# Own-block masks on two engines, and a new order, in a four-layer attention kernel

## The chip, the cores and the metric

The kernel runs on one core of a Trainium2 chip. The core has TensorE (PE, with a weight loader that the profile lists as PEld), VectorE (DVE), ScalarE (ACT), GpSimd (POOL) and SyncE (SP, which here only issues DMAs); they run side by side and meet through semaphores. The metric is the time of one execution on the device in microseconds (us). Before the change three runs gave a median of 410.37 us (410.02 to 410.41).

## The reference

The input has 2048 tokens of 512 features in bfloat16. Four residual layers follow each other: A, B, A, B, all with 32 heads of 16 features, and each with a layer normalisation ahead of it.

```
x = x + A(layernorm(x), A_wqkv, A_wo)      # twice, in turn with
x = x + B(layernorm(x), B_wqkv, B_wo)

A: phi(t) = where(t > 0, t + 1, exp(t)) + 1e-6
   kv = sum_s phi(k)_s v_s ;  z = sum_s phi(k)_s
   o = phi(q) kv / (phi(q) z + 1e-6) ;  o @ wo

B: scores = q k^T * 16^-0.5, kept where 0 <= i - j < 256, else -1e9
   o = softmax(scores) v ;  o @ wo
```

A is linear attention over the whole sequence: nothing can be read from it before all keys have been summed. B is causal attention over a window of 256 tokens. A score outside the window ends as a probability of zero, and these zeros are what the changed lines make.

## The kernel before

**Tiles.** Tokens are cut into 16 tiles of 128. The residual `xres` stays on the chip through all layers. Matrix products go into the eight banks of the accumulator `PS` (`ps` in the profile), and ScalarE or VectorE bring them out.

**Stages.** `layer_a_keys` builds the first layer's key sums; `barrier` closes a linear layer; `middle(2)` runs the end of the first A layer, the first B layer and the start of the second A layer tile by tile; a second `barrier` follows; `middle(3)` runs the end of the second A layer and the second B layer, and stores the result. Inside a `middle` the steps of tile j+3's projections, tile j's scores and tile j's values stand side by side.

**A normalisation** (`norm`) is a chain over engines: mean and variance on VectorE (L367, L368), an epsilon added on GpSimd or VectorE (L369), the power -1/2 on GpSimd (L370), the normalised tile on VectorE (L371), then a transpose, mostly by a DMA of SP's queue (L377), and then the projections on TensorE (L406, L420), whose results are evicted by ScalarE or VectorE (L395, and L591/L592 for the keys). In the linear layers the exponential of `phi` is ScalarE's (L429) and its clamp and join are VectorE's (L430, L431).

**A sliding-window tile.** `b_scores` is called four times for each key tile j: for two halves b of 64 keys and two groups of feature blocks `fs`. TensorE multiplies the keys with up to 256 queries (L638), in four row groups of 32 and four banks; ScalarE takes the exponential of two banks at a time into the probabilities `pb` (slots in `vp` in the last stage) (L648). The first 64 queries of each such block overlap the keys' own positions, so part of them must be zero: the mask `mk` does this, by a product with the 0/1 triangle `tri` on VectorE (L656), in place, over 8 head rows of 64 columns for 128 keys. `b_far` treats the 64 queries at the window's far end (L677, L680 on TensorE, L690 on ScalarE); its mask `mf` covers 16 head rows and is made by VectorE's product (L709) or by GpSimd's `affine_select` (L708), which writes zeros where an affine function of partition and column is negative. In the last B layer (`merged`) the own and far blocks of tiles 0 to 13 share their columns; there the own mask is made in `b_far` on VectorE (L700), and `b_scores` masks only tiles 14 and 15. `b_values` multiplies the probabilities with the values (L729) for three key tiles at a time; it reads `pb` after all masks. Its sums are divided (L740, L741), transposed and projected, and added to the residual (L574).

**The order.** Nothing is ordered at run time. `Plan` lists 2542 operations with their dependences and, for some, the engines that may run them (`g.add(name, {engine: cost, ...})`). `place` unpacks `TABLE`, which holds three things found by a search made beforehand: a place in the order for every operation, the engine of every operation, and the accumulator bank of every tile. Each engine then plays its operations in that order and waits at each on semaphores of the others. `place` also adds waits: a bank's new user waits for the old ones, and a longer GpSimd operation waits for the last VectorE operation of the kinds in `WIDE` that stands before it:

```
SHORT = ("eps", "pow", "c2", "c2b", "c11", "c12", "c13", "c14")
WIDE = ("E1", "xn", "mk", "mf")
...
        if o.eng == "POOL" and o.name not in SHORT and wide and wide not in o.deps:
            o.deps.append(wide)
        if o.eng == "DVE" and o.name in WIDE:
            wide = o
```

`synchronise` lets every GpSimd operation wait for the one before it on GpSimd. Output stores `outp` (L847) go through SP's or GpSimd's queue, as the table says. Ten matrix products without use (`fill`, L268) and nine more at the very start (L984) keep TensorE busy while the first tiles come in.

Of the kernel before, what the change touches and what calls it, by code (L numbers as in the profile page):

```python
# [218 lines left out]
def bass_view(x, free):  # L219

    return bass.AP(x.tensor, x.offset, [x.ap[0]] + free)


class Plan:
# [398 lines left out]
    def b_scores(self, j, b, fs, key):  # L623

        K = self
        ps = [Tile(1, "S") for _ in range(4)]
# [15 lines left out]
        sl = j % self.rp  # L642
# [8 lines left out]
        if skip:  # L651
            return

        def mk(e):
            x = bass_view(K.P(sl)[:, fs[0], 0, 384 * b:384 * b + 64], [[704, 4 * n], [1, 64]])
            return e.tensor_tensor(x, x, K.tri[:, 0, :].unsqueeze(1).to_broadcast([P, 4 * n, 64]), ALU.mult)  # L656
# [200 lines left out]


TABLE = (
    r"c-qZa1K1|VvaT*P*0yciwr$(CZQHhO+qTW@CcDXcb7%hV<eVfoo0F4!@AKUGhSk+o?^{*fGyMUCh3765goc+c9E6835CI|rLPAiG2oggihztY|-3#}`C",  # L860
    r"4r=n43a|>hzijl3kWoa6p#`avO+fK1uY;ujD@Ez2SkS$&>LDpE9e8oAQe1v8a6_D$N)JZ7i0tjaUd=@c<fq38+hjCLu%LreIXx=gZ!`=YC|392gRX3jE",
    r"8s-6Ba;xXbbJY!USjp?I9C9aCKn-420Zp80tY9=m1@zK6Hc3&>dnyIY<i)AUHIJK`<CP!bC^_O<)o%ghj9zmcUi$1Y4j7Y=t3k1dhTn*aop79W;b4Py#",
    r"x`WOxo!U?>cOGEf$#LQi-BFJUPxgXItmuE7^L4%guZOoQoA9lpZPumWzvN{Fjw!EBfV!=XHU2d|(4Y=<4N6L!H|m;p0kHSC5}a023~lW+<^DHU4HgD@(",
    r"-N}%?_Ew~MLpedY&Gw>S1syz@+B~;(TS-1;7z#BLZ;Z=H72~d$@RTG*)26YbZ!F?D3BViO&1yK*+Eo4-gR3epF{Rlrn1Qk(5QUz5ZRaj+KSyU3G)k84K",
    r"s>rH{DypKWf=~#mKvb1fy@O;bxpFGH8VzHhw#urqsbVU-%Aty@5~`$%rgEyvkW!^kxl}1tTIE({RaI3@l~Gkx0jQ($KwhY;>Zt~*vZ}6XsFtdgYOQLjT",
    r"B^QU18ZR&6ow*D6xyhUs;z3I8mo4yiE6K!tBTN6HB&9rde{Ip-~#M}{cr#}sDm(CjZq=s5j=*uYM!bFW7Rk{QjJm<VVxSU)~iEM5+<mLYQDMzlhgur85",
    r"XJ|s-xPVp1@O>tlq;1n4)H=nQE3=q&BL>YKfYvrm5+wlez+%)Mm9`9aRU^QuPcvt1fDeI;OU$t?Hm!sk*9<uu9c})vBB7u0FvswOj?m;J8A~R=3n~6#|",
    r"2);OdSl1t-)=bxQS6Au$wQRoB#QbzN;!C9ouZhSMs9I;;+<N9wUEh1*p~6-t%H&=>}HsGaJGx~ZaL42+4-)C<*9mBF&OOYK(A)jf4zmBTZtmkNt})LB&",
    r";o~m=|fm)+3sEg{nTB~AX0!)Mn@uez{XYirAq-tU<ysK`gI2aG(Vr@K&=WrCB#|wB7M`IEkgYj{nN`|RaYV}UNS0B_H^-;Z5KdPTpQcR8^AsnVr;V}Y^",
    r"#c?<uBVt;W0uy5etcaDcGVWE8FeRo_bulug!i*RN>){oZ2`{S&I1w9Q6|9Q&F*9bt)OZPF;bp9Y)$o&QhAnV5&cV6Z96zf`_(gqHKP$jS*ch{7Hq4GW@",  # L870
    r"Gf4#?^Hv)hxf4wHpN#;AtK>xH5q?UQ*bJ_!mHQ@b7E_}hS#y2`d;-`jOA5Zte`5YN-7Q3z+9LXJ7X8@iVH9uw#0>)8@pk5%z$|?FXlr*jZrZ_7QjUq4H",
    r"u(9i%YNv&PRvKuqRH#7-}h|$CxUX>V*YyIZnqJ7+b|rE3go*!mYRsx8n|6iG5UGRUOyhIxLL+)Bx2RS7U!w1jEr<T#rSu7>1_^R2(BxB#KP)@EJbG7kC",
    r"4A;x62cd+-N*gEz4<RiU?d3m@SVe29;+5B9~ExEG^PRLY~OQa_AFc~yTLfcaE@)ebx0U7CdhaS%Sm0_q;M$4)pHhv1JGpAt|)x=#buAoU%-#u?NRXJR#",
    r"~PBo||?Zf@}3OC?Jyn_dDCVj%sIEyyn_qYXXQ40EkUvW0gp`Q^bB`HEmMX4zX#iH1hjN;Hx9ENGAHXX#Il$?g+2poy&XfAEW=oEuuQhjPb4=@8A!ozq3",
    r"(^5{#MYpjbJ)lhVkXlkkBFas9s1+rmN0gqJgftz+%(Rl)QXLwsT2mWpPl@RmKBgzMidIuQ>Oeo?dwhrSs4mr`yp)gf(+4a-9jOU5rB2kD3X-9&)Sa5qa",
    r"Xf(^@g#Pm=G2eYQGc38mK+76`LuxI(kVQR184&Ur$RK4TF`nbOkHRb^`IgYf{Icx8bpI>Ej^_nw3&v|7Ro|dX)6_{5>%2F(jr<+*=PxEqwTbmcF;1~NF",
    r"gZ{4N)W1P?eoRQy3~mKhPT*uHMoxwTpIB4%$PBI58*Tq@0Y`P-!YdWhpF`qsCO8l5+~~NiV4vrQ~NcjC#{|G@M4zNE$_r=oRgw*R-Gd&~y5p4$~2OL8I",
    r"v?9is#EiN4Sp9z$bkFYTnYypEgmJNiuTX&il}7Tl5#Q7S%8<LLyQq!08n0r&M@8mH(qt>?^~g@2-~oSJ{6kJO4=a~md3!)aNVIRuB~P@IF?a!wA-nhz3",
    r"kE<QtN=^UM>c07S5QXUS&VR;fwrYV$;^Ko7d$KkmM=jIEvfs1i|UQX$`D6gOl{3HLw@3=h|;6i+nE>UsL#+RuqZ{$rJfy;4cF3%OXAQ$G%+?Ts>f9}9t",
# [36 lines left out]


# [153 lines left out]
```

## Time and profile before

| | |
|---|---|
| median of 3 runs | 410.37 us |
| span of the profiled execution (the page gives no other time of it) | 408.2 us |
| TensorE busy | 396.0 us (97%) |
| VectorE busy | 347.9 us (85%) |
| ScalarE busy | 344.4 us (84%) |
| GpSimd busy | 113.8 us (28%) |
| own-block masks on VectorE (L656) | 72, 0.42 us each |
| far masks on GpSimd (L708) / on VectorE (L709) | 39 at 1.15 us / 17 at 0.69 us |

A row of the groups reads: line, engine, operation, what it writes `<-` what it reads (buffer numbers left out), shapes, count | busy us, mean ns of one | idle time of its engine just before these instructions, and which engine's work ended it. A row of the waits reads: who waited `<-` for whom, us in total, times, longest. A piece of the chain is its start, its length and what ran. The span runs from the first to the last instruction; matmul ends are modelled, so a busy TensorE may still have short gaps. Granted clock is 1.00 in every stage.

### The profile page before, as it was taken

To read this page: it belongs to the slowest core of one execution; us is meant where nothing else is said; L and a number is where in the kernel's file an instruction comes from. 1 tells how busy PE (TensorE), PEld (TensorE's weight loads), DVE (VectorE), ACT (ScalarE), POOL (GpSimd) and SP (SyncE) were. 2 spreads that over 40 slices of the span, in tenths; PEclk is the share of its full clock that TensorE was granted. 3 is DMA by queue.
4 is the path that set the end of the run, shared out by engine and by line. 5 is a ranking of instruction groups with operands and counts; after the bars stand their busy time and mean duration, and the time that the engine had idled before them with its cause. 6 is when DMAs were issued, how large, how long until landed. Compare 5 with 4: busy or idle time off the path is not lost.

```text
span 408.2 us, 18082 instructions
## 1 busy us (share of the span) xinstructions
PE 396.0 (97%) x7997; PEld 263.4 (65%) x7997; DVE 347.9 (85%) x808; ACT 344.4 (84%) x443; POOL 113.8 (28%) x194
## 2 busy tenths in 40 slices
PE   8999999999999999999999999999999999999996
PEld 3654676666575566666666777676757766576664
DVE  5998799999998999888977789988898778876685
ACT  3655579999999999999998355999998999999992
POOL 3553632112253343330503202122123201302212
PEclk9999999999999999999999999999999999999999
DMA  8754014923242934344231100364225542442543
GB/s 247 243 118 104 2 42 121 184 56 97 65 119 52 132 73 108 75 104 106 62 69 36 29 2 28 89 127 78 71 76 130 143 83 61 66 121 62 118 109 104
DMA packets 67654, 37.88 MB, mean 93 GB/s; under 512 B 48248, under 2 KB 62712, under 8 KB 67576
## 3 DMA queue, kind: packets, MB, share of 16 engines
q1 hardware_dynamic: 67184, 35.67, 38.1%
q8 instruction: 63, 1.03, 1.1%
q0 software_dynamic: 384, 1.05, 0.8%
q14 instruction: 15, 0.12, 0.1%
q10 hardware_dynamic: 8, 0.00, 0.0%
HBM read 6.29 MB, written 2.10 MB: 21 GB/s over the span
## 4 chain that ended last, share of the span: by engine, by line
PE 81%; ACT 10%; DVE 7%; DMA 1%; issue 1%; DVEq 0%
PE ps L406 27%; PE ps L420 20%; PE ps L729 15%; PE ps L638 8%; ACT pb L648 7%; PE ps L680 2%; PE ps L481 2%; ACT pb L690 1%; DVE XQ L563 1%; PE ps L677 1%; DMA XQ<-vp 1%; PE ps L984 1%; PE ps L457 1%; PE ps L543 1%; PE ps L268 1%
## 5 line engine op out<-in xcount | busy, mean ns | idle before, releaser
L648 ACT ACTIVATE pb<-ps 128x1024 bf16<-128x1024 f32 (+3 forms) x224 | 198.2, 966 | 7.4 <-PE ps L638 6.2
L729 PEld LDWEIGHTS ps<-vB,pb 128*128 128x128 bf16 x2560 | 77.6, 96 | 11.5 <-issue 4.2
L729 PE MATMUL ps<-vB,pb 128*128 128x34 bf16 x2560 | 83.2, 177 | 0.3
L420 PE MATMUL ps<-xT,wBp 128*128 128x128 bf16 x1024 | 68.6, 219 | 0.1
L420 PEld LDWEIGHTS ps<-xT,wBp 128*128 128x128 bf16 x1024 | 58.4, 98 | 9.6 <-issue 4.0
L708 POOL TENSOR_SCALAR_AFFINE_SELECT pb<-pb 128x1024 bf16<-128x1024 bf16 x34 | 39.1, 1149 | 84.0 <-DVE pb L700 31.9
L429 ACT ACTIVATE tE<-ps 128x512 bf16<-128x512 f32 x64 | 38.1, 606 | 18.4 <-PE ps L406 12.1
L638 PE MATMUL ps<-XQ,kB 32*128 32x256 bf16 (+2 forms) x1024 | 48.7, 262 | 3.3 <-ACT pb L648 0.6
L574 DVE TENSOR_TENSOR xres<-ps,xres 128x512 bf16<-128x512 f32 x63 | 43.1, 685 | 9.6 <-PE ps L406 9.1
L690 ACT ACTIVATE pb<-ps 128x1024 bf16<-128x1024 f32 x50 | 49.0, 1048 | 1.3 <-PE ps L680 1.0
L406 PE MATMUL ps<-wA,XQ 128*128 128x512 bf16 x192 | 49.2, 380 | 0.7 <-DMA XQ<-vp 0.6
L369 POOL TENSOR_SCALAR ve<-mv 128x1 f32<-128x1 f32 x49 | 11.8, 240 | 127.9 <-DVE mv L368 126.9
L370 POOL TENSOR_TENSOR rs<-ve,negh 128x1 f32<-128x1 f32 x64 | 37.9, 592 | 32.0 <-DVE ve L369 27.5
L367 DVE BATCH_NORM_STATS2 stats<-xres 128x6 f32<-128x512 bf16 x64 | 43.8, 685 | 2.8 <-DMA xres<-in_A_x_dram 2.1
L638 PEld LDWEIGHTS ps<-XQ,kB 32*128 32x128 bf16 x1024 | 15.7, 92 | 31.4 <-ACT pb L648 8.3
L420 PE MATMUL ps<-XQ,wA 128*128 128x128 bf16 x512 | 34.4, 219 | 0.0
L406 PE MATMUL ps<-wBv,xT 128*128 128x512 bf16 x128 | 34.3, 380 | 0.0
L406 PE MATMUL ps<-M,XQ 128*128 128x512 bf16 x128 | 33.3, 380 | 0.2
L420 PEld LDWEIGHTS ps<-XQ,wA 128*128 128x128 bf16 x512 | 30.1, 98 | 5.1 <-issue 0.6
L406 PE MATMUL ps<-wBo,oT 128*128 128x512 bf16 x124 | 32.7, 380 | 0.6 <-DVE vp L431 0.4
L656 DVE TENSOR_TENSOR pb<-pb,tri 128x512 bf16<-128x512 bf16 x68 | 27.7, 419 | 3.7 <-ACT pb L648 3.1
L741 DVE TENSOR_TENSOR o<-ps,rc 128x256 bf16<-128x256 f32 x64 | 27.0, 422 | 1.7
(114 smaller groups left out, 545.9 us busy)
## 6 DMA issues: line engine op xcount, KB each, us to landing
vB<-vS SPq DMA_DIRECT2D x64, 136.0 KB, 2.6
kB<-vp SPq DMA_DIRECT2D x64, 128.0 KB, 2.2
wA<-in_A_wqkv_dram SPq DMA_DIRECT2D x3, 512.0 KB, 5.2
xres<-in_A_x_dram SPq DMA_DIRECT2D x2, 512.0 KB, 4.8
pb<-in_B_wqkv_dram SPq DMA_DIRECT2D x1, 1024.0 KB, 6.9
out_dram<-xres POOLq DMA_DIRECT2D x8, 128.0 KB, 2.5
out_dram<-xres SPq DMA_DIRECT2D x7, 128.0 KB, 2.0
xres<-in_A_x_dram SPq DMA_DIRECT2D x3, 256.0 KB, 5.3
```

The costliest lines, as they stand in the source:

```text
L367: self.on("DVE", "stats", lambda e: e.bn_stats(K.stats[:, t, :], K.xres[:, t, :]), key, dve(512), rd=[("xres", t)], wr=[("stats", t)])
L370: self.pow = self.on("POOL", "pow", lambda e: e.tensor_tensor(K.rs[:, t, :], K.ve[:, t, :], K.negh[:], ALU.pow), key + 0.03, (640, 690), r ...
L406: m = e.matmul(K.ps(ps), lhs(c), rhs(c), start=c == 0, stop=c == 3)
L420: m = e.matmul(K.ps(ps)[:, f * P:(f + 1) * P], w(c, f), xT(c), start=c == 0, stop=c == 3)
L429: self.on("ACT", "E", lambda e: e.activation(K.tE[:, s, :], K.ps(ps), ACT.Exp, bias=0.0), key, act(512), wr=[("tE", s)], ps=[ps])
L574: self.on("DVE", "res", lambda e: e.tensor_tensor(K.xres[:, t, :], K.ps(po), K.xres[:, t, :], ALU.add), key, dve(512), rd=[("xres", t)], w ...
L638: m = e.matmul(K.ps(ps[gq])[:, ns * i:ns * i + ns], K.kB[rows, j % 4, 2 * f + b, :, :], K.XQ[rows, f, q:q + ns], start=True, stop=True, ti ...
L648: return e.activation(out(h, ns).rearrange("p (f g) c -> p f g c", f=n), i, ACT.Exp, bias=0.0, scale=0.25)
L656: return e.tensor_tensor(x, x, K.tri[:, 0, :].unsqueeze(1).to_broadcast([P, 4 * n, 64]), ALU.mult)
L690: return e.activation(o.rearrange("p (f g) b c -> p f g b c", g=2), i, ACT.Exp, bias=0.0, scale=0.25)
L708: return e.affine_select(out=x, in_=x, compare_op=ALU.is_ge, fill=0.0, base=-2, pattern=[[0, 16], [-2, 64]], channel_multiplier=1)
L729: m = e.matmul(K.ps(ps)[:, 34 * u:34 * u + 34], K.P((b // 2) % rp)[:, f, gq % 2 * 2 + gq // 2, o:o + P], K.vB[:, (b // 2) % 4, b % 2, r, : ...
```

## The change

The mask `mk` of `b_scores` may now be made on GpSimd too: there it is an `affine_select` in place, which keeps an element of the block where 1 + 2 x column - partition is not negative and writes 0 elsewhere, over the same 8 x 64 columns. Which engine makes a mask is read from the table, as for `mf`. The search's cost for it is 600 ns on GpSimd. The 56 own masks of `b_far` stay on VectorE.

The table is a new one: it has other places in the order, other engines for those operations that may go to several, and other banks. 50 of the 72 masks of `b_scores` go to GpSimd (46 of 64 in the first B layer, 4 of 8 in the last). Other operations that change engine: far masks (6 more on VectorE in the first B layer, 3 fewer in the last), epsilon adds, some evictions, a few clearings and weight copies of the start, and 2 output stores that go from SP's queue to GpSimd's. 439 of the 1007 accumulator tiles get another bank.

```diff
@@ b_scores
-        def mk(e):
+        def mk(e, eng):
             x = bass_view(K.P(sl)[:, fs[0], 0, 384 * b:384 * b + 64], [[704, 4 * n], [1, 64]])
+            if eng == "POOL":
+                return e.affine_select(out=x, in_=x, compare_op=ALU.is_ge, fill=0.0, base=1, pattern=[[0, 4 * n], [2, 64]], channel_multiplier=-1)
             return e.tensor_tensor(x, x, K.tri[:, 0, :].unsqueeze(1).to_broadcast([P, 4 * n, 64]), ALU.mult)
 
-        self.on("DVE", "mk", mk, key + 0.02, dve(256 * n, "2x"), rd=[("P", sl, f, b, h) for f in fs for h in range(2)] + [("tri",)], wr=[("P", sl, f, b, 2) for f in fs])
+        self.g.add("mk", {"DVE": dve(256 * n, "2x"), "POOL": (600, 660)}, mk, key + 0.02, rd=[("P", sl, f, b, h) for f in fs for h in range(2)] + [("tri",)], wr=[("P", sl, f, b, 2) for f in fs])
@@ TABLE
...
```

More of the change, by code (lines that the diff above doesn't have):

```diff
@@ L864 @@
[L864 to L879, printed above, removed]
@@ new lines @@
+    r"76gOZPzU-#KS%{_pe-DPb}$agKwTIQ?V&Stfv(UW2EZX$05M@8Y=AUSA3DGw*a$ITA#{Vma2QfUJ=g@B;Ujc{jxYp<!V!oA6Cf^hhly|*Ccz?D4DnzIOomU8",
+    r"2lB#axB^pP25f<?unmsFQkV%-VLEJwS@0B&!Bw~hm0=k?gXb^}Uchy@0m~tzdI>uKlv4Si0W^e_uoI5M2{;KW;3nLHP%5^%4X5B0po*hTLuj=dW<wYiR^5R)",
+    r"unX=&5hx17U^t{z`BfvR24|rZ#8vTB0Z69`LVT58y@odsPQ8V9K&lvMRUYm`0rdl9P^=QDGjI=#`Vqpbj4Fbv0K?T!5K)P;s-Q}!8bcvfSTzBsBB{tKkxHyG",
+    r"smv;iilRn9R+U60RYg=$RZJCEQB`s^5~@Nrm0cxMIaCQ%Qsso4s<bKxl~pNKNmWsyp{6Pgqo9_mt?H<Xs;a7{3PC;9T(wZuRSnfrt%B9C2691eC=9JsUDZ~t",
@@ new lines @@
+    r"h1RN}YNV<_eN`43sB_R%HCF4OojMO~R5R5?U4V<Q2lm29HA<C$lCTf<!)!H2jZmXibr_=_z(bg;#;S2@ys89;)M0f1=Bb}yf?A{2s`+Z7dJmVNy?O)-)IzmR",
+    r"EmDisBsEQSP}9{6HA_{5^=hWttB$D0&{6GElhuATMQu=>)CZWVp1=~dR4r2*)h5+NEmtelO0`*SQC(GMby@uaSJVx4R9#iKR5x`@9alHi3H2)kQ9)HO6$FD~",
+    r"F}$rFs7ERoo>W^^4LG2Js}QO<mcZb+O<h+H)pivXqhSa<sJg4iDmp$<*VHq$L+w;OR7os_tJEnK5?8C!DmdIxrSYkXfxFZhbynR~_tZI62FqehEQjaS1r-nP",
+    r"tDdSl*1%Jk0Apb&42?DMG={-5I0B!mkvIzDV?rE_DO4Oxgt74~rc`n9tvZMA)DNl_UQ|D+pVfQyK_$V&m`a7kaF`4uU_?BRKdSIp9xGsSOo3x?ERMrHsv_=I",
@@ new lines @@
+    r"zo^tIjY^M^@B&`MI#>_u;w4oZ>thD2gq1NPX2S8<1ZUzb{8fEaO)(`_!P(dh8(>5Hq&};pm>C-(U>3ZMS@DI+hIjBTzErQ2LPWv|I1wk|WNd*gu{pk0t?&|F",
+    r"#w*ww->5R`Dwb8{R4Po3X)ql&#`3BocESp39xlMnm>qNAd`yd7Fem21+?WURVm{Q!Xi#twF2SxCO<8mp1@mJ!?2e0Z3NFOxDu(KTQ*kLq#%UN+#Zt>~1un<U",
+    r"xCMKut+*1mVQ;kx`>6t05Z7QK?1`%}427k>YA*IsRWTeD#<lnapJEX#is2~&UBm6T1E1j=ypB6@7gnT7^cJh(4Sa`l@Hsxfhgg}a&=2?sdtq<vgMG0d=2E#;",
+    r"9u<)yQDka^?Ql27rFfKARi%6?3f-m|IF0(Nd)OZb;6SWK15{h=fRFJ7-l6Gqm*P`<oI%y;6~4sRxChtadfbcqa6kTn8*n53ipeNBeZ<fB34u0YBC0`y@Bkjf",
@@ new lines @@
+    r"6qJ$_Atk0mI2~h9Oo~N=aR|<&S(JqC<50YXsVEIarD!yp=Fl)4jy0(+)uW^ool;X;x{38E9o?h*^ni#CV|L0w=_w=Spq$j4T2KPg#FUE+C8U<ridxfhT0w2;",
+    r"2-c!D)Q(otj~JWc(9c+#>X1-w%0oY4Udl)LsXcX|qu7y-;c@It@3AX&p+?l0EIA57AFvP2r4x7(=g~kFl!8$c>PCHO4XvYQ)Q|d80V+s^s41<b4YZLu(Eu7q",
+    r"t7ttHrXp07Hc=+ZOvPvr4W=P9pNi80T1XG+5oMu8w1pPa63R+jX&Y^)H}sa?(I6F^2CEQMf_6|y8m5M*p=uZHq->NxC)9~_V!fG?=%hNCE=i^6F*TslRE8Q-",
+    r"cj`gU=>>(NC-jtt(n~5!J?R<kp<#584pDL)no{WDG=dJ(UK&ZSXdnGTAE_6urd7H(HPuJxS8AqzqMvCuHP@qPG>xILv|6vxN9h=SrnUMwouHGnPOsPR$$LrY",
@@ L915 @@
+    r"Kl*$Mit(RI_JuxF-?VSmqZELMzly+%?l%U}fOsJQ`#yZMzSzU*=gQOe{6ir6FM;}m`|Vgz2LvC8(AW3oS^2j<7lD5KX>SI#(q4+#kD1X6hsCQG_Q~=fdI=}v",
+    r"1?F9dR-QXe=wl_t+8CczKlMIXAGYrx5Qk^XOT1Sj{-rMngbo21{BXs`9~jN=3HKa&ZoMP~)Qt)}2U<W9-z;#TF@LS^$!F2K2lluK$W>rczf_Cz3f%uJfxt`$",
+    r"`U_m60v}!wU-L`-eOc>MPJZEf0drs>1gdy33V8k?Fi(NV0+D)2@?3c|2ZkA#W#6fvbKjo&QaXNJ{KmguBjSGv=r5)JdtC*X4yZHVN?`T;_5gU)egPZ^-;V{=",
+    r"Z)N@EDI_0>F9n}u{vVVdGBE",
 )
```

73 lines of the change are left out of this document (34 added, 39 removed).

## The prediction

> **What bounds the kernel.** I read the page first, its shares of engines and the chain, then the busy times by stage, then the chain piece by piece, and last the waits.
>
> ```profile
> span 408.2 us, 18082 instructions
> PE 396.0 (97%) x7997; PEld 263.4 (65%) x7997; DVE 347.9 (85%) x808; ACT 344.4 (84%) x443; POOL 113.8 (28%) x194
> PE 81%; ACT 10%; DVE 7%; DMA 1%; issue 1%; DVEq 0%
> ```
>
> The chain that ended last is 81% TensorE. The stages in turn (columns: length, busy time with instruction count for PE, PEld, DVE, ACT, POOL, then clock, DMA share and GB/s); 60 to 225 is the first sliding-window layer ("the second stage" below), 260 to 400 the last one:
>
> ```profile
> 0.00:60.00 60.00, 58.07 (x564) 34.10 (x565) 52.23 (x128) 32.26 (x54) 26.96 (x66) 1.00 0.45 126
> 60.00:80.00 20.00, 19.98 (x312) 13.54 (x310) 19.24 (x44) 18.84 (x24) 4.34 (x11) 1.00 0.71 153
> 80.00:220.00 140.00, 137.94 (x2898) 88.90 (x2896) 124.19 (x292) 136.84 (x160) 43.29 (x62) 1.00 0.39 85
> 220.00:260.00 40.00, 39.90 (x637) 28.83 (x636) 34.21 (x75) 22.39 (x41) 8.20 (x16) 1.00 0.13 32
> 260.00:400.00 140.00, 135.41 (x3492) 94.68 (x3489) 114.11 (x263) 132.57 (x165) 28.65 (x39) 1.00 0.42 93
> 400.00:408.20 8.20, 4.72 (x111) 3.34 (x109) 3.93 (x9) 1.46 (x4) 2.38 (x5) 1.00 0.42 130
> ```
>
> TensorE and ScalarE are both close to full in the two sliding-window stages; VectorE, which the change relieves, is third. TensorE's idle time can be read off stage by stage: 1.9 us to 60, 0.0 to 80, 2.1 to 220, 0.1 to 260, 4.6 to 400 and 3.5 in the tail. That is all that a better order could take out, since the changed program issues the same 868 TensorE steps. Two stretches of the chain show both limits:
>
> ```profile
> 1.25 4.02 PE ps L984 x9
> ...
> 115.54 3.77 ACT pb L648 x4
> 119.80 7.39 ACT pb L648 x8
> 127.19 1.83 ACT pb L690 x2
> 129.02 2.75 ACT pb L648 x3
> ...
> 143.76 0.34 PE ps L677 x32
> 144.11 1.45 PE ps L420 x24
> 145.56 0.86 PE ps L406 x4
> 146.42 0.34 PE ps L677 x32
> ```
>
> From 143.76 each TensorE piece begins where the one before it ends; at 115.5 to 131.8 it is the exponentials, with no mask between them. The busy time of a matmul counts its modelled tail, so short gaps don't show in the stage sums; I allow 3 us for these (an estimate of mine: the loader's waits below come in pieces of up to 0.7 us), which makes at most 2.1 + 4.6 + 0.7 + 3 = 10.4 us to be had, the 0.7 being what of the first 60 us is not the first 1.25 us before any work.
>
> **The change part by part.** In the changed program 50 of the 72 own-block masks are GpSimd selects, 46 of the 64 in the second stage and 4 of the 8 in the last. The order and engine choice of everything else comes from a new table too.
>
> ```profile
> L656 DVE TENSOR_TENSOR pb<-pb,tri 128x512 bf16<-128x512 bf16 x64 | 26.0, 418 | 3.5 <-ACT pb L648 3.1
> L708 POOL TENSOR_SCALAR_AFFINE_SELECT pb<-pb 128x1024 bf16<-128x1024 bf16 x24 | 27.6, 1151 | 44.2 <-ACT pb L690 19.1 <-DVE tE L430 10.3 <-DVE pb L656 8.3
> L328 POOL TENSOR_SCALAR_AFFINE_SELECT spread<-spread 128x512 bf16<-128x512 bf16 x4 | 3.4, 848 | 0.6
> L334 POOL TENSOR_SCALAR_AFFINE_SELECT tri<-tri 128x64 bf16<-128x64 bf16 x1 | 0.2, 238 | 1.1 <-DVE tE L430 1.1
> L709 DVE TENSOR_TENSOR pb<-pb,tri 128x1024 bf16<-128x1024 bf16 x4 | 2.7, 682 | 0.0
> L592 DVE CAST vp<-ps 128x512 bf16<-128x512 f32 x25 | 18.3, 730 | 4.3 <-PE ps L420 3.9 <-DMA kB<-vp 0.3
> L591 ACT ACTIVATE vp<-ps 128x512 bf16<-128x512 f32 x7 | 5.3, 755 | 2.6 <-PE ps L420 2.6
> L395 ACT ACTIVATE XQ<-ps 128x512 bf16<-128x512 f32 x10 | 6.0, 597 | 1.2 <-PE ps L420 0.8
> L369 DVE TENSOR_SCALAR ve<-mv 128x1 f32<-128x1 f32 x15 | 2.2, 149 | 0.3
> L847 POOL DMA_DIRECT2D out_dram<-xres x8 | 4.7, 594 | 22.3 <-DVE xres L574 13.8 <-DVE vp L656 5.5 <-DVE pb L700 3.0
> ```
>
> Masks off VectorE: 46 x 0.418 = 19.2 us less in the second stage, 4 x 0.418 = 1.7 us less in the last.
>
> Price of a select of 512 elements: not in the trace in this form. It lies between 0.24 us (64 elements) and 1.15 us (1024); the one row of 512 elements, with another pattern, has 0.85. A line through the two ends gives 0.24 + 448/960 x 0.91 = 0.66 us, and I take that, because the row of 1024 has the same kind of pattern and tile. GpSimd gets 46 x 0.66 = 30.4 us there (39 at the row of 512).
>
> Masks of the far blocks: 6 more go to VectorE in the second stage (+4.1 us there, 6.9 us off GpSimd), 3 fewer in the last (2.0 us off VectorE, +3.5 on GpSimd).
>
> Small moves in the second stage: 6 epsilon adds to VectorE (+0.9); key evictions, two more on VectorE (+1.5) and off ScalarE (-1.5); query evictions, one the other way (-0.7, taken at the key's size; +0.6 on ScalarE). Sum: VectorE -19.2 + 4.1 + 0.9 + 1.5 - 0.7 = -13.4 us, ScalarE -0.9 us, GpSimd about +22 us on the 52 it has there, still under half of 165. In the last stage VectorE loses about 5 us, ScalarE gains 1.4 us for two evictions (they stand near 274 and 311, where it is 1.2 us in 20 idle) and a 1.2 us clearing before it. Two output stores move from SP's queue to GpSimd's, at 0.59 us of it each, all but the last of them long before the end.
>
> The order: engine by engine, 693 of TensorE's 868 steps and 367 of ScalarE's 442 keep their relative order, and a TensorE step shifts by 1.2 places on average; TensorE changes between full and split arrays 333 times in both. So TensorE's work costs nothing more or less, and what can change is only its idle time.
>
> What covers the longer mask? The waits of TensorE's loader and of GpSimd, between 60 and 225 us (columns: total, times, longest):
>
> ```profile
> PEld ps L638 <- ACT pb L648: 5.1, 11, 0.7
> PEld ps L729 <- DVE pb L656: 1.0, 4, 0.3
> ...
> POOL ve L369 <- DVE mv L368: 54.0, 17, 9.4
> POOL pb L708 <- ACT pb L690: 19.1, 6, 6.1
> ```
>
> The probability-times-value matmuls (L729) waited four times for a mask, at most 0.3 us, so most masks are done early and 0.24 us more (0.66 against 0.42) is hidden; without that cover 46 x 0.24 = 11 us would show. GpSimd has the room: it sat 54 us waiting for nothing but the next mean and variance.
>
> The sum for the path: of the 2.1 us of idle TensorE in 80:220 I take half to go, since VectorE is the third engine there and loses 10% of its load; of the 3 us of hidden gaps 0.7; of the 4.6 us in 260:400 only 0.8, because the relief there is small and the last part of that stage runs on exponentials; against it 0.6 us for selects that hold VectorE up. -1.0 - 0.7 - 0.8 + 0.6 = -1.9 us. The profiled span of 408.2 becomes 406.3; the median of the runs, 410.37, stands 2.2 us above the span, and I keep that: **408.5 us**.
>
> **A row against the relief.** GpSimd and VectorE have held each other up once in plain sight:
>
> ```profile
> 37.57 0.85 POOL L328 TENSOR_SCALAR_AFFINE_SELECT spread<-spread 128x512 bf16<-128x512 bf16 x1
> ...
> 37.65 0.92 DVE L430 TENSOR_SCALAR tE<-tE 128x512 bf16<-128x512 bf16 x1
> ...
> L430 DVE TENSOR_SCALAR tE<-tE 128x512 bf16<-128x512 bf16 x64 | 18.4, 292 | 2.4 <-ACT tE L429 2.0
> ```
>
> The clamp of L430 takes 0.29 us on average and took 0.92 when it began 0.08 us after a select: a loss of 0.63 us. After the change GpSimd selects for 46 x 0.66 + 18 x 1.15 = 51 us of the 165. [...]
>
> **Rivals.**
> - *Hidden anyway.* VectorE holds only 7% of the chain, and the two full engines keep their work. Then TensorE's idle time stays: 410.3 us. Against it: 13.4 us is a lot for an engine at 89% in 80:220.
> [...]
> - *Slower: GpSimd's queue.* The power of each normalisation stands in the same queue as the selects, and a select at its head has waited up to 6.1 us for exponentials. With 46 more of them, a normalisation that comes 1 us late in four places delays the transposed input, and so the projections: 410.4 + 4 = 414 us. Against it: 54 us of waiting in that queue.
>
> **How the numbers follow.** About 0.2% (0.8 us) is what a measurement of this kernel tells from no change. Forecast 0.50, hidden 0.14, port 0.22, queue 0.14; so faster 0.50, within 0.2% 0.14, slower 0.36. The forecast's own range is 405 (half of all that is to be had) to 409.5. The range for all: 405.0 leaves out the best few per cent, 414.0 the worse half of the queue's case and more than one hold-up in ten on the path: 405.0 to 414.0.
>
> **What would show it.** Right: VectorE's busy time down to about 330 us, GpSimd's up to some 140; selects of 512 elements at 0.6 to 0.7 us; TensorE's idle time in 80:220 under 1.5 us; L729 not waiting for GpSimd by more than 1 us in sum. [...] The queue: normalisations (L371) waiting for GpSimd's power for more than the present 0.7 us in that stage. I am wrong if TensorE's idle time grows in a stage that has no selects: then the new order as a whole did it, not the masks.

## The result, and the profile after

The changed kernel takes 415.29 us (median; 412.63 to 417.36), before 410.35 (409.33 to 412.71) beside it. The ratio is 1.0114, 95% interval 1.0084 to 1.0143: slower by about 1.1%. The forecast was 408.5 us, and 414.0 was the upper end of the range.

From the page of the changed kernel: span and instructions, the busy times, the chain, and the group of the new selects.

```profile
span 414.8 us, 18073 instructions
PE 388.5 (94%) x7923; PEld 263.8 (64%) x7997; DVE 341.0 (82%) x766; ACT 344.5 (83%) x443; POOL 144.6 (35%) x238
PE 65%; DVE 14%; ACT 10%; DMA 5%; issue 3%; SPq 1%; POOL 1%; POOLq 0%
L657 POOL TENSOR_SCALAR_AFFINE_SELECT pb<-pb 128x512 bf16<-128x512 bf16 x48 | 32.1, 670 | 68.1 <-ACT pb L648 47.8
```

The select costs 0.67 us (0.66 was taken) and GpSimd is as busy as expected (144.6 us). VectorE's busy time fell by 7 us only, to 341, where about 330 was expected. The chain is 65% TensorE instead of 81%; VectorE and DMAs have taken the rest. 74 matmul records are missing in this trace, so TensorE's busy time can't be read from it. The weight loads (PEld) are complete, 7997 in both.

So I measured the loss by them. The 868 TensorE steps are the same in every kernel here; each step's first weight load has a start in each trace, and the table gives that start less the start in before's trace, as a median over the steps of 10 us of before's time (us; minus is ahead of before).

| at | after | loads late (e1) | two hold-ups mended (m1) | power mended too (m2) |
|---|---|---|---|---|
| 20 | +3.1 | -0.1 | +0.2 | -0.5 |
| 60 | +2.4 | -0.8 | -0.6 | -1.2 |
| 150 | +2.6 | -0.5 | -0.3 | -0.5 |
| 170 | +3.7 | +0.5 | -0.2 | -0.4 |
| 210 | +4.7 | +1.6 | +0.9 | +0.7 |
| 230 | +3.7 | +0.6 | -0.2 | -0.4 |
| 350 | +3.9 | +0.8 | +0.5 | +0.1 |
| 370 | +5.4 | +1.1 | +0.8 | 0.0 |
| 390 | +6.0 | +2.6 | +2.5 | +1.5 |

Read down a column: 3 us are lost before the first select, nothing is gained in the 90 us from 60 to 150 that hold 24 of the 46 selects of that stage, 2 us are lost between 150 and 215 and one of them won back, and 2 us are lost behind 350. The experiments (the other columns) take these stretches one by one. Two profiled executions of the same order differ by up to 0.8 us in such a column: at 60, where e1, h1, h4, m1 and m2 still share the order, they stand between -0.6 and -1.4. So only steps within a column are used, and the timed results beside them.

### The profile page after: what moved, and what is told of

Its sections match the earlier page's. It is cut to its first block, busy times and chain, and to the rows that moved or that the text cites. A ratio compares the mean times of both kernels' runs of the same rounds, so it can differ in the third digit from the quotient of the medians.

```text
span 414.8 us, 18073 instructions
## 1 busy us (share of the span) xinstructions
PE 388.5 (94%) x7923; PEld 263.8 (64%) x7997; DVE 341.0 (82%) x766; ACT 344.5 (83%) x443; POOL 144.6 (35%) x238
## 4 chain that ended last, share of the span: by engine, by line
PE 65%; DVE 14%; ACT 10%; DMA 5%; issue 3%; SPq 1%; POOL 1%; POOLq 0%
PE ps L406 22%; PE ps L420 17%; PE ps L731 11%; ACT pb L648 7%; PE ps L638 6%; ACT pb L692 2%; PE ps L481 2%; PE ps L682 2%; DMA xres<-in_A_x_dram 2%; DVE xres L574 1%; DVE stats L367 1%; DMA XQ<-vp 1%; DVE XQ L563 1%; DMA xT<-xn 1%; PE ps L457 1%
## 5 line engine op out<-in xcount | busy, mean ns | idle before, releaser
L420 PE MATMUL ps<-xT,wBp 128*128 128x128 bf16 x1024 | 69.6, 219 | 2.1 <-DMA xT<-xn 1.4
L657 POOL TENSOR_SCALAR_AFFINE_SELECT pb<-pb 128x512 bf16<-128x512 bf16 x48 | 32.1, 670 | 68.1 <-ACT pb L648 47.8
L406 PE MATMUL ps<-wA,XQ 128*128 128x512 bf16 x180 | 47.6, 390 | 4.6 <-DMA XQ<-vp 2.2
L710 POOL TENSOR_SCALAR_AFFINE_SELECT pb<-pb 128x1024 bf16<-128x1024 bf16 x32 | 37.2, 1163 | 36.8 <-DVE pb L711 12.6
L420 PE MATMUL ps<-XQ,wA 128*128 128x128 bf16 x512 | 35.5, 219 | 0.1
L406 PE MATMUL ps<-wBv,xT 128*128 128x512 bf16 x106 | 29.5, 380 | 2.6 <-issue 1.6
L406 PEld LDWEIGHTS ps<-wA,XQ 128*128 128x128 bf16 x192 | 16.9, 99 | 23.1 <-issue 3.2
L406 PE MATMUL ps<-M,XQ 128*128 128x512 bf16 x116 | 30.3, 380 | 1.0 <-issue 0.3
L742 DVE RECIPROCAL rc<-ps 128x16 f32<-128x16 f32 x64 | 15.8, 249 | 18.7 <-PE ps L731 18.2
```

The source lines that it names most:

```text
L406: m = e.matmul(K.ps(ps), lhs(c), rhs(c), start=c == 0, stop=c == 3)
L420: m = e.matmul(K.ps(ps)[:, f * P:(f + 1) * P], w(c, f), xT(c), start=c == 0, stop=c == 3)
L657: return e.affine_select(out=x, in_=x, compare_op=ALU.is_ge, fill=0.0, base=1, pattern=[[0, 4 * n], [2, 64]], channel_multiplier=-1)
L710: return e.affine_select(out=x, in_=x, compare_op=ALU.is_ge, fill=0.0, base=-2, pattern=[[0, 16], [-2, 64]], channel_multiplier=1)
```

## The experiments

The order of an experiment is the table's, with operations moved; everything else is the changed kernel's or the old kernel's code. Lines of after stand two further down than before's from L657 on; in e1 and e3 they are four further down than in after, in e4 two.

### The loads of the first stage

SP's queue between 12 and 31 us, before and then after (columns: start, us, instruction):

```profile
17.03 3.91 SPq L377 DMA_TRANSPOSE XQ<-vp  x3
20.98 0.59 SPq L286 DMA_DIRECT2D wAo<-in_A_wo_dram  x1
22.77 7.75 SPq L377 DMA_TRANSPOSE XQ<-vp  x5
```

```profile
12.17 0.51 SPq L286 DMA_DIRECT2D wAo<-in_A_wo_dram  x1
14.64 0.37 SPq L290 DMA_DIRECT2D wBv<-in_B_wqkv_dram  x1
16.62 4.46 SPq L377 DMA_TRANSPOSE XQ<-vp  x3
```

The new table loads two weights of 0.5 MB, needed much later, ahead of the first transposes; before they stood behind three of them and behind all. The chain of after in this stretch:

```profile
16.62 5.87 DMA XQ<-vp
22.53 3.50 PE ps L406 x8
26.48 0.86 PE ps L406 x4
```

The first transpose lands 5.87 us after its issue, and TensorE waits. Then it is slow as well: eight matmuls of 512 columns take 3.50 us, 0.44 each, where four take 0.86 (0.22 each) later. The wait is on this row:

```profile
22.53 3.50 PE L406 MATMUL ps<-wA,XQ 128*128 128x512 bf16 x8 [2.25 <-DMA XQ<-vp]
```

The granted clock of 20:40 is 0.91 here, 1.00 before (columns as in the stage rows of the prediction):

```profile
20.00:40.00 20.00, 17.64 (x110) 9.05 (x111) 16.09 (x43) 10.54 (x16) 9.33 (x22) 0.91 0.37 61
```

Within this stretch it is 0.50 from 22.40 to 25.81 us, over nearly all of the eight: half rate, as their 0.44 us have it, behind a wait of 2.25 us.

Two kernels test this, one putting the loads back into the new order and one putting them forward in the old one:

```diff
 e1: after's order
-wAo, wBv, transposes 1..11
+transposes 1..3, wAo, transposes 4..11, wBv
 e2: before's order
-transposes 1..3, wAo, transposes 4..11, wBv
+wAo, wBv, transposes 1..11
```

> The changed kernel with the two loads wAo and wBv put back to their old places in SP's queue (behind the third and behind the last of the first layer's transposes); masks stay on GpSimd. Loads theory (the first transposes queue behind 1 MB of weights, TensorE waits 2.3 us and its clock falls to half for 3 us, 1.6 us lost): 3 to 4 us faster than the changed kernel's 415.3, so 411 to 412.5, and 200 to 250 GB/s at most in 12 to 20 us. Masks theory (the selects cost the time): stays at 415. Whole-order theory (many small things): 414 to 415.

> The kernel before with the same two loads moved ahead of all transposes of the first layer, as the change has them; nothing else. Loads theory: 3 to 4 us slower than before, 413.5 to 414.5, with a wait of TensorE for a transpose near 20 us. Masks theory and whole-order theory: 410 to 411.

Measured: e1 412.57 us, ratio 1.0053 (1.0032 to 1.0074); e2 412.25 us, ratio 1.0041 (1.0009 to 1.0073). The first transposes in their chains:

```profile
18.37 3.43 DMA XQ<-vp
```

```profile
16.55 6.13 DMA XQ<-vp
22.72 1.04 PE L410 MATMUL ps<-wA,XQ 128*128 128x512 bf16 x4 [2.46 <-DMA XQ<-vp]
```

With the loads out of the way (e1, first row) the landing takes 3.43 us and the wait is gone; with the loads forward the old order has the same 6 us (e2, the other two rows) and a wait of 2.46 us. That wait is longer than the changed kernel's, but no half rate follows it (four matmuls in 1.04 us, granted clock 1.00), so the length of the wait alone (2.25 and 2.46 us) does not explain the clock here. e2 was expected to lose 3 to 4 us and loses less. So the loads' place alone is worth 1.7 us in the old order and 2.5 in the new one (ratios 1.0114 and 1.0053), of a loss of 4.7 us, and it has nothing to do with the masks.

### The masks with the old places, and the new places without the masks

```diff
 e3: before's order, 50 own masks
-VectorE: tensor_tensor(x, x, tri, mult)
+GpSimd: affine_select(x, x, ...)
 e4: after's order, the same 50 masks
-GpSimd: affine_select(x, x, ...)
+VectorE: tensor_tensor(x, x, tri, mult)
```

> The kernel before with the same 50 own-block masks on GpSimd, at their old places in the order; nothing else. Loads theory: the masks are hidden, 409 to 412 (an order not searched for them may lose 1 us by the queue). Masks theory: 413 or more.

> The changed kernel with all own-block masks back on VectorE at their places in the new order. Loads theory: 414 to 418, no gain, since the loss of the first 25 us stays. Masks theory: 411 to 412. Whole-order theory: 415.

Measured: e3 417.48 us, ratio 1.0165 (1.0119 to 1.0212); e4 443.25 us, ratio 1.0792 (1.0751 to 1.0833). One row of TensorE's waits in each, values for masks:

```profile
PE ps L735 <- POOL pb L661: 2.3, 4, 0.8
```

```profile
PE ps L733 <- DVE pb L660: 5.6, 6, 1.5
```

Both times lie outside what the loads theory expected (409 to 412 and 414 to 418), and e3's is one that the masks theory allowed (413 or more). Each order fits its own engines for the masks: with the other engine the probability-times-value matmuls wait for masks. e3 shows the selects not hidden where the order doesn't provide for them (four waits, 2.3 us in sum), and VectorE's masks, normalisations and clamps are held up there for another 4.1 us in sum, as in the section on the hold-ups below; the waits of TensorE in after name GpSimd nowhere, those of its loader once (0.3 us). e4 says nothing about the price of a product against that of a select, only that the new places count on GpSimd's queue; TensorE's waits for these masks are 5.6 us of its loss of some 33, and the rest was not taken apart.

### The stages one by one

Pieces of both orders were put together (the new order here always with late loads):

```diff
 h1: -before            +new to 87 us, then before
 h2: -before            +before to 70 us, new to 238 us, then before
 h3: -before            +before to 262 us, then new
 h4: -before            +new to 87, before to 215, new to 238, then before
```

> The first 590 of the 2542 operations (to about 87 us) stand in the new order with the new engines, but with the two first-layer weight loads put back behind the transposes; all later operations stand in the order, engines and banks of before. Theory 'loads, then a sum of small things': the new first stage without its early loads is itself a little better than the old one; at 87 us the trace of the run with the loads put back was 0.6 to 0.8 us ahead of before, so 409.7 us, ratio 0.998. Rival 'the new order is worse all along': ahead of nothing, 410.4 us or more.

> Before's order for the first 470 operations (to 70 us) and behind operation 1535 (about 238 us); between them the new order with its 46 selects on GpSimd. Only the stage of the masks is new. Theory 'the masks' stage gains nothing': between 70 and 238 us the trajectory of the run with the loads put back lost 1.3 us net (+2.4 to 215 us, -1.0 after), so 411.7 us, ratio 1.003. Rival 'the selects help, the loads and the last stage ate it' (my forecast's own sum for this stage): 408.7 us, ratio 0.996. Rival 'the selects alone are the loss': 412.5 us or more.

> Before's order for the first 1680 operations (to about 262 us), the new order behind them, with its 4 selects among the last 8 own masks, its two output stores on GpSimd's queue and its late normalisations. Theory 'the last stage costs on its own': the trajectory of the run with the loads put back went from +0.7 to +2.6 us in this stretch and lost 0.4 in the tail, so 412.5 us, ratio 1.005, with a gap of over 1 us inside a group of probability-times-value matmuls near 385 us and a transpose of about 4.9 us near 362. Rival 'those losses are carried over from the stages before': 410.4 us, ratio 1.000.

> The pieces of both orders that were ahead in the trajectories, put together: the new order with late loads to operation 590 (87 us), before's to 1405 (215 us), the new one to 1535 (238 us), before's for the rest; 8 of the own masks are selects. Theory 'the stretches add up': -0.7 us of the first piece and -1.0 us of the third, so 408.7 us, ratio 0.996. Rival 'a gain in one stretch is given back at the next full engine': 410.0 us or more, ratio 0.999 or more.

| | us | ratio, 95% |
|---|---|---|
| h1 | 410.11 | 0.9981 (0.9960 to 1.0002) |
| h2 | 413.66 | 1.0065 (1.0047 to 1.0083) |
| h3 | 413.06 | 1.0062 (1.0039 to 1.0085) |
| h4 | 410.54 | 0.9999 (0.9982 to 1.0015) |

The new first stage without its early loads is as good as the old one or slightly better. The stage of the masks alone costs (h2), by its time as much as the rival "the selects alone are the loss" had it (412.5 or more); but of its shift of 3.0 us half sits at the two joints, where the pieces don't fit (0.95 us near 65 and 0.54 near 240), which my 411.7 had left out; the other half repeats the steps of e1 between 150 and 230. All matmul records of h2 are there, so its busy time can be compared with before's 137.94 in that window:

```profile
80.00:220.00 140.00, 136.76 (x2839) 88.81 (x2836) 119.72 (x262) 134.57 (x157) 62.17 (x91) 1.00 0.37 83
```

VectorE is busy for 4.5 us less (the window also holds 60 weight loads fewer) and TensorE is idle for 3.2 us instead of 2.1. The last stage costs by itself too (h3). h4 shows that the stretches don't add up, as its rival had it: its trace loses 0.95 us at the joint near 210, wins 0.6 and loses 0.5 again at the joint near 240, so the piece that won 1.0 us in e1 is worth nothing between pieces of the other order.

### VectorE held up beside GpSimd's selects

VectorE's groups between 60 and 225 us, two of before, where the mask L656 has a mean of 418 ns, and then three of after:

```profile
L371 DVE TENSOR_SCALAR xn<-xres,mv,rs 128x512 bf16<-128x512 bf16 x27 | 10.8, 399 | 0.8 <-POOL rs L370 0.7 <-DMA XQ<-xn 0.2
L430 DVE TENSOR_SCALAR tE<-tE 128x512 bf16<-128x512 bf16 x20 | 5.8, 288 | 1.2 <-ACT tE L429 1.1
```

```profile
L371 DVE TENSOR_SCALAR xn<-xres,mv,rs 128x512 bf16<-128x512 bf16 x27 | 12.9, 476 | 0.4 <-POOL rs L370 0.3
L658 DVE TENSOR_TENSOR pb<-pb,tri 128x512 bf16<-128x512 bf16 x15 | 7.7, 516 | 1.6 <-ACT pb L648 1.6
L430 DVE TENSOR_SCALAR tE<-tE 128x512 bf16<-128x512 bf16 x22 | 7.1, 326 | 1.0 <-ACT tE L429 0.8
```

27 x 0.077 + 15 x 0.098 + 22 x 0.038 = 4.4 us more for the same work, nearly all of it in ten operations. Two places, GpSimd's rows and then VectorE's:

```profile
176.11 1.15 POOL L710 TENSOR_SCALAR_AFFINE_SELECT pb<-pb 128x1024 bf16<-128x1024 bf16 x1
...
201.23 1.30 POOL L710 TENSOR_SCALAR_AFFINE_SELECT pb<-pb 128x1024 bf16<-128x1024 bf16 x1 [0.82 <-ACT pb L692]
202.60 0.72 POOL L657 TENSOR_SCALAR_AFFINE_SELECT pb<-pb 128x512 bf16<-128x512 bf16 x1
203.39 2.42 POOL L710 TENSOR_SCALAR_AFFINE_SELECT pb<-pb 128x1024 bf16<-128x1024 bf16 x2
```

```profile
176.07 1.33 DVE L371 TENSOR_SCALAR xn<-xres,mv,rs 128x512 bf16<-128x512 bf16 x1 [0.28 <-POOL rs L370]
177.32 0.67 DVE L395 CAST vS<-ps 128x512 bf16<-128x512 f32 x1
...
201.44 1.36 DVE L658 TENSOR_TENSOR pb<-pb,tri 128x512 bf16<-128x512 bf16 x1
202.72 0.74 DVE L430 TENSOR_SCALAR tE<-tE 128x512 bf16<-128x512 bf16 x1
203.50 0.69 DVE L431 SCALAR_TENSOR_TENSOR vp<-ps,tE 128x512 bf16<-128x512 f32 x1
204.11 0.57 DVE L430 TENSOR_SCALAR tE<-tE 128x512 bf16<-128x512 bf16 x1
```

The normalisation of 0.40 us takes 1.33 and ends at 177.40, 0.14 us after the select; the mask of 0.42 us takes 1.36, and two clamps behind it 0.74 and 0.57. L431 and L395, which read the accumulator, keep their 0.69 and 0.67 us beside selects; none of their 22 and 33 in this stretch takes more than 0.70. The normalisation's record begins 0.04 us ahead of the select that holds it up; a clamp of k1 below begins as much ahead of its select and is not held up, so starts as close as this don't tell which of two operations waits. 'The port', also 'the shared port', is the author's name for these hold-ups in the recorded texts; whether the two engines share anything of that kind, no run shows.

The search's new order has waits of selects for the VectorE operation ahead of them, but nothing keeps the next VectorE operation off a select that is already running. In the table above the losses of e1 stand right behind such places (near 160, 174 and 198 to 210 us). To test this, selects were moved back behind the operation that they had held up; they then wait for it:

```diff
 k1: e1's order, 18 selects at 10 places and in the last stage; m1: 4 selects at the first two
-select A, select B, ..., xn (held up)
+..., xn, select A, select B
```

> The new order with the loads put back (412.57 us, ratio 1.0053), and 18 selects on GpSimd moved a few places back in the order, each behind the normalisation, clamp or mask on VectorE that took 0.2 to 0.9 us too long beside it. Engines and all other places stay. Theory 'the shared port': the trajectory of the run with the loads put back lost 0.4 us near 160, 0.6 near 174 and 1.1 between 198 and 210 us, each right behind such a hold-up; these 2.1 us go, so 410.5 us, ratio 1.000, and the longest mask, clamp and normalisation in 60:225 take under 0.6 us. Rival 'the places of the tiles, not the port': the waits move but the sum stays, 412.5 us.

> The first 1535 operations (to about 238 us) of the new order with late loads and moved selects, 46 of them masks of the second stage; before's order behind them. Theory 'with the loads, the port and the queue out of the way the selects are worth something': -0.8 us to 87 us, about -0.3 more to 225, so 409.3 us, ratio 0.997, the best of all. Rival 'VectorE's relief is worth nothing on the path': no better than the first stage alone with late loads, 410.1 us, ratio 0.998 or more.

> The whole new order with all three changes: late loads, moved selects, the power ahead of the far select. If the three causes add up: 412.57 - 2.1 - 0.5 to 1.1 = 409.4 to 410.0 us, ratio 0.997 to 0.999. If a cause is still missing (the rest of the last stage): 410.5 us or more, ratio 1.000 or more.

> The new order with the loads put back (412.57 us, ratio 1.0053), and only four selects moved, each pair behind the normalisation that was held up for 0.6 us near 158 and 0.9 us near 173 us. Theory 'the shared port': the 1.0 us that the trajectory loses between 150 and 180 us go, and nothing else changes: 411.5 us, ratio 1.003. Rival 'the loss is in the tiles' places, the hold-ups are hidden': 412.5 us, ratio 1.005, the trajectory loses the same at 160 and 175.

Measured: k1 420.33 us, ratio 1.0229 (1.0201 to 1.0258); k3 419.88, 1.0209 (1.0178 to 1.0240); k4 419.81, 1.0218 (1.0190 to 1.0245). My mending was wrong: TensorE's waits in k1 begin with

```profile
PE ps L731 <- POOL pb L710: 4.8, 1, 4.8
PE ps L731 <- POOL pb L657: 1.7, 4, 0.7
```

A far select near 88 us, put behind a mask that comes later, got behind another far select that waits 4.04 us for its exponentials, and kept the value matmuls waiting for 4.8 us. All hold-ups of the second stage but two of 0.12 and 0.07 us were gone in k1, and the loss between 150 and 190 us with them (k1 moves by 0.1 us there, e1 by 1.0), but the total shows only that the slack of a select is small.

k3 has k1's order up to 238 us, and its trace holds a test that nobody planned. GpSimd's select and VectorE's clamp near 165 us, in k1 and then in k3, and TensorE's next wait in k3:

```profile
165.08 1.26 POOL L710 TENSOR_SCALAR_AFFINE_SELECT pb<-pb 128x1024 bf16<-128x1024 bf16 x1 [0.89 <-ACT tE L429]
165.04 0.29 DVE L430 TENSOR_SCALAR tE<-tE 128x512 bf16<-128x512 bf16 x1
```

```profile
165.38 1.15 POOL L710 TENSOR_SCALAR_AFFINE_SELECT pb<-pb 128x1024 bf16<-128x1024 bf16 x1 [0.89 <-DVE xn L371]
165.45 1.23 DVE L430 TENSOR_SCALAR tE<-tE 128x512 bf16<-128x512 bf16 x1
167.46 0.40 PE L638 MATMUL ps<-XQ,kB 32*128 32x256 bf16 x8 [0.59 <-DVE vp L431]
```

In k1 the clamp begins 0.04 us ahead of the select and keeps its 0.29 us; in k3 it begins 0.07 us behind it and takes 1.23. From 150 to 170 us k3 falls behind by 1.0 us and doesn't win it back up to 230, while k1 and k4 stay within 0.1 there. The order is the same in all three, and the clamp is what is held up in one of them only: the loss is the hold-up's.

m1 moves only the four selects near 160 and 174 us. Its rows, GpSimd and then VectorE:

```profile
173.23 1.15 POOL L710 TENSOR_SCALAR_AFFINE_SELECT pb<-pb 128x1024 bf16<-128x1024 bf16 x1 [0.52 <-DVE xn L371]
```

```profile
172.74 0.41 DVE L371 TENSOR_SCALAR xn<-xres,mv,rs 128x512 bf16<-128x512 bf16 x1 [0.28 <-POOL rs L370]
173.09 0.69 DVE L395 CAST vS<-ps 128x512 bf16<-128x512 f32 x1
```

The select waits 0.52 us, the normalisation takes 0.41 us again, and the column m1 is flat from 150 to 170 (-0.3 to -0.2) where e1 loses 1.0. The time is 411.95 us, ratio 1.0043 (1.0021 to 1.0066): 0.4 us less than e1 by the ratios, and that alone would not tell them apart; the traces do, at the place. Most of the gain is gone again further on: m1 is 0.8 us ahead of e1 at 230, 0.3 at 350 and 0.1 at 390. The third place (198 to 210 us, about 1.1 us) was not mended without a new wait, and is put down to hold-ups by its rows only; k1, with new waits and no hold-up there, loses 1.9 us from 190 to 210.

### GpSimd's queue in the last stage

GpSimd between 349 and 363 us, in before, in h3 (the new last stage) and in k2:

```profile
352.12 0.22 POOL L369 TENSOR_SCALAR ve<-mv 128x1 f32<-128x1 f32 x1 [2.00 <-DVE mv L368]
352.43 0.57 POOL L370 TENSOR_TENSOR rs<-ve,negh 128x1 f32<-128x1 f32 x1
```

```profile
351.20 0.57 POOL L369 TENSOR_SCALAR ve<-mv 128x1 f32<-128x1 f32 x1 [4.63 <-DVE mv L368]
359.07 1.15 POOL L710 TENSOR_SCALAR_AFFINE_SELECT pb<-pb 128x1024 bf16<-128x1024 bf16 x1 [7.30 <-DVE pb L711]
360.30 0.57 POOL L370 TENSOR_TENSOR rs<-ve,negh 128x1 f32<-128x1 f32 x1
```

```profile
351.91 0.57 POOL L370 TENSOR_TENSOR rs<-ve,negh 128x1 f32<-128x1 f32 x1
359.46 1.15 POOL L710 TENSOR_SCALAR_AFFINE_SELECT pb<-pb 128x1024 bf16<-128x1024 bf16 x1 [6.98 <-DVE xn L371]
```

In h3, as in after, a far select stands between the epsilon and the power of one normalisation and waits 7.30 us; the power comes at 360.30 instead of 352.43, the normalised tile and its transpose follow, and TensorE waits for the transposed input. k2 puts the power ahead of the select:

```diff
 k2: h3's order; m2: m1's order
-eps, far select, ..., far mask, bqe, rcp, div, xn
+eps, pow, far select, ..., far mask, xn, bqe, rcp, div
```

> Before's order to operation 1680 and the new last stage behind it, as in the run of the new last stage alone (413.06 us, ratio 1.0062), with one pair changed: the power of one normalisation is put ahead of a far select in GpSimd's queue that stood there from 352 to 360 us, waiting for its exponentials, and the normalised tile of VectorE goes back accordingly. Theory 'GpSimd's queue': the transposed input is then issued some 3 us earlier, the wait of 1.2 us of TensorE at 365 us goes, so 411.9 us, ratio 1.0034. [...]

> The same, and the power of the normalisation near 352 us ahead of the far select in GpSimd's queue. If the mended causes add up: 0.3 to 0.9 us less than the run before this one, 410.6 to 411.2 us, ratio 1.001. Rival 'what is saved before is given back at the next full engine': as the run before it.

Measured: k2 412.16 us, ratio 1.0025 (1.0004 to 1.0047), against 1.0062 of h3; m2 411.51 us, ratio 1.0014 (0.9997 to 1.0031), against 1.0043 of m1. The same TensorE step in h3 and in k2:

```profile
366.31 1.05 PE L420 MATMUL ps<-xT,wBp 128*128 128x128 bf16 x16 [1.14 <-DVE pb L702]
```

```profile
365.17 1.07 PE L420 MATMUL ps<-xT,wBp 128*128 128x128 bf16 x16
```

The wait of 1.14 us is gone (the profile puts it down to a mask that ended last; in after it names the transpose, 1.4 us). The output stores stayed where they were, so they are not its cause. The timing alone would not show it: the intervals overlap in both pairs, and by the medians, each less that of before beside it, the power is worth 0.4 and 0.8 us. m2 is the new order with the three mended causes, 50 masks on GpSimd and all: not told from before.

### What stays open

In the group of value matmuls at 390 us TensorE stops for more than a microsecond, waiting for nothing that the profile shows. In after:

```profile
390.39 0.18 PE L731 MATMUL ps<-vB,pb 128*128 128x34 bf16 x1
391.90 0.24 PE L731 MATMUL ps<-vB,pb 128*128 128x34 bf16 x3 [1.33 <-issue]
```

It isn't the new order's: every kernel run here has it between the 7543rd and the 7553rd of the 7997 weight loads, in the value group or in the score group right behind it, with a step of 0.6 (before), 0.8 (k3), 0.9 (h1), 1.0 (e3), 1.1 (k2), 1.2 (e2) and 1.5 us (after). Up to 0.9 us of the difference between the two profiled spans is this gap. The traces tie it in time to a queue that the profile lists as one of instructions, with 63 packets of 16 KB, in after's page as (packets, MB, share of 16 engines):

```profile
q8 instruction: 63, 1.03, 1.0%
```

In all 16 traces the 59th of these packets starts as TensorE comes to its weight loads 7501 to 7516, and TensorE goes on 1.25 to 1.52 us after that packet's end, whether its stop had begun early or late. No run moves the packet: that TensorE waits for it is the author's reading and was not shown, and why it would wait at this one is open.

The steps at 390 in the columns e1, m1 and m2 are larger than the stop, because the granted clock falls again some 2 us behind it. m2's row, where before, after, h1 and k2 have 1.00:

```profile
380.00:400.00 20.00, 17.54 (x464) 12.00 (x462) 13.14 (x31) 17.36 (x23) 5.76 (x8) 0.91 0.46 102
```

It doesn't happen in every execution: a mean granted clock under 0.997 is on record for 19 of the 34 timed runs of e1, m1 and h3, 8 of the 24 of k2 and m2, 8 of the 44 of e2, e3, h1, h2 and h4 (the old last stage), and 8 of the 88 of before that were timed beside them; it is also on record for all 22 of e4, k1, k3 and k4, the four slowest, of which k3 has the old last stage. In the first three groups the kernels with the new last stage have it more often; why was not tested. The last 0.4 us, a slower tail (4.18 us from the start of the last matmul to the end against 3.75), was not tried.

## Why the prediction was wrong

- **What failed: "The order".** It said that TensorE's work "costs nothing more or less, and what can change is only its idle time", from the relative order of TensorE's and ScalarE's steps, and then put nothing into the sum for a loss by the new places; of the DMAs only the two output stores were counted. The other queues had changed more: in the longest common order TensorE keeps 702 of its 868 steps, but VectorE 510 of the 731 that stay on it, GpSimd 109 of 159 and SP 144 of 229. In SP's queue two loads had moved ahead of the first transposes: 2.5 us, the largest single item, in a stage without a select. In GpSimd's queue one power had moved behind a select that waits 7 us: 1.2 to 1.5 us by the ratios (m2 against m1, k2 against h3), 0.4 to 0.8 by the medians, 1.1 by the trace of k2. And TensorE's work did cost more: eight matmuls ran at half rate (0.44 instead of 0.22 us each) behind the wait for the first transpose.
- **"Wrong if TensorE's idle time grows in a stage that has no selects"**: it did, in the first one, and at once.
- **The masks off VectorE**: 13.4 us less were expected in the second stage. Over the operations of that stage (60 to 225 us in before), matched one by one, the durations on VectorE sum to 163.5 us before and 156.0 after: 7.5 less. The count was right but for one value eviction more (0.7 us); the other 5.1 us went into hold-ups, 2.2 in masks, 2.1 in normalisations and 0.8 in clamps.
- **The price of a select**: right (0.67 against 0.66), and hidden in the new order (TensorE's loader waits for GpSimd once, 0.3 us). The cover is thinner than "L729 waited four times" suggested: at the old places four waits of up to 0.8 us appear (e3).
- **The gain from the relief (1.0 + 0.7 + 0.8 us)**: not there. From 60 to 150 us, with half of the selects, the shift doesn't move. TensorE and ScalarE are both full there, which fits that an engine that was third gives nothing. That was the first rival, and m2, with the mended causes, ends where that rival put it (410.3): ratio 1.0014. But m2 still has 3.9 us of hold-ups on VectorE, and no kernel here has the selects without either the hold-ups or new waits of selects, so a small gain that the hold-ups eat is not ruled out.
- **The 0.6 us "for selects that hold VectorE up"**: mis-sized. It was the author's estimate, with one hold-up in the trace before (0.63 us on L430), and no run shows 0.6 us; the chance of 0.22 for "port" stood for more of them on the path. What the runs showed in its place: 5.1 us on VectorE, nearly all in some ten operations, with L430's mean at 326 ns instead of 288. Where they stand, two places cost the path 1.0 us (m1 against e1) and the one of k3 another 1.0; how much of that reaches the end is not shown (0.4 us by the ratios of e1 and m1, less than their intervals tell apart).
- **The queue**: this rival's mechanism was real, once instead of four times, and in the last stage, with a far select and not an own one. In the second stage its sign stayed away: L371 waits 0.3 us for the power, not more than 0.7.
- **Two small readings**: GpSimd had 49.7 us of work in 60 to 225 us, not 52. And the two output stores are a net count: six went to GpSimd's queue and four came back.

In ratios of before: 0.6% for the loads, which the intervals of after and e1 tell apart; about 0.3% for the power's place and 0.1% for two hold-ups, which the traces show at their places and the timing alone doesn't. Together they are 1.0% of the 1.1% (after against m2), and what is left can't be told from nothing. Three small causes of different kinds came together with a gain that did not show.

## What to carry to other kernels

When a change brings a new order, compare every queue with the old one, the DMA issues and the helpers' queues first, and not just the steps of the full engine: here two loads moved forward made more than half of the loss, and one short operation behind a long wait came next. Relief of an engine that was third, while two others were full, brought nothing that could be measured. Where GpSimd is given long operations (here selects of 0.67 and 1.15 us), list what VectorE starts while they run (here single ones took up to 0.94 us longer); moving the long one behind the short one helps only where its result has time to spare (in k1 one that had none kept TensorE waiting for 4.8 us).

## What had not been expected

A wait of 2.25 us of TensorE was followed by eight matmuls at half speed (0.44 instead of 0.22 us for one of 512 columns, granted clock 0.50), so the early loads cost more than the wait itself; a wait of 2.46 us in e2 was not. A transposing DMA behind two loads of 0.5 MB landed in 5.9 to 6.1 us instead of 3.4. VectorE's masks, normalisations and clamps were held up to the end of a GpSimd select plus 0.14 to 0.27 us, up to 0.94 us each, while L431 and L395, which read the accumulator, took 0.70 us at most; between k1 and k3 a shift of 0.11 us between the two starts decided who waits. And TensorE's stop near the 7550th weight load is in every kernel, whatever the order, from 0.6 to 1.5 us long, and ends 1.25 to 1.52 us after the same packet of instructions.
